# Two large gathers moved to the head of GpSimd's queue, and two more early groups with an announced jump

## The chip, the cores and the metric

One Trainium2 chip; the kernel runs on one of its cores. The metric is the device time of one execution in microseconds, the median of repeated runs. The engines are TensorE (PE, with PEld for its weight loads), VectorE (DVE), ScalarE (ACT), GpSimd (POOL) and SyncE (SP), which issues most of the DMAs.

## The reference, cut to what matters

Three stages follow one another. Attention (2 batches, 8 heads, 768 positions, 64 wide) gives 1536 tokens of 512 numbers. A mixture of experts works on these: a token with a positive skip score goes to the one expert of eight that its gate prefers, the others pass unchanged. A feed-forward block of 2048 hidden columns works on all tokens.

```python
do_compute = x @ w_skip > 0                  # tokens that go to an expert
e_idx = np.argmax(xc @ w_gate, axis=1)       # one of 8 experts each
h = np.maximum(xc[mask] @ w1[e], 0.0)        # 512 -> 1024
y[mask] = gate_w[mask, None] * (h @ w2[e])   # 1024 -> 512
out[do_compute] = xc + y
h = x @ w_in                                 # 512 -> 2048, all 1536 tokens
out = (h * np.cos(h)) @ w_out                # 2048 -> 512
```

## The kernel before

Attention writes its 1536 rows to a table `xb` in DRAM. The stage of the experts reads its rows from there and writes them back in place, and the feed-forward block reads the finished rows from there.

**Experts.** `CAP` is 32. The first 32 tokens of every expert are gathered as a small tile `xg` (`ex_gather`, 64 half rows). The next up to 64 are a tile `xo` (`ov_gather`, 64 rows), which is gathered for every expert whether it has them or not. An expert with more than 96 tokens has, instead, a tile `xm` of 128 rows (`many_gather`), which stands under a condition, since few experts are so large; one with more than 160 has both. All of these are indirect DMAs of GpSimd, which its queue issues in the order of the program. The weights (2 MB for each of an expert's two matrices, in four pieces) go through eight buffers; SyncE issues the pieces in order, each behind the landing of the third piece before it, and those ahead of the loop behind one gather each (`load_piece(ex_gather(...))`).

The loop over the experts is staggered: iteration `e` turns the hidden rows of expert `e` (`ex_t`), makes the first product of expert `e + 1` (`ex_w1`), turns the rows of expert `e + 2` (`ex_x`), then makes the second product of `e` (`ex_w2`), adds and scatters its rows (`ex_out`), and runs the larger tiles of `e` under their conditions (`overflow`, with `full_tile` for 128 rows and `part_tile` for 64). For every condition each engine reads the count into a register and branches.

**Work between the experts.** The table `WORK` puts steps of the next stage into the loop, under a letter for the place (`B` ahead of the second product, `J` behind the overflow, `A` behind that) and the number of the expert. Steps are named `c` (join the two halves of a weight chunk into float32, on ScalarE and VectorE), `sp` and `s` (split it into two parts for the product; the cast is on ScalarE, the subtraction on GpSimd for `sp` and on VectorE for `s`), `l` (load one), `yl` and `y` (gather 128 finished tokens and transpose them), and `f`, `b`, `d`: the three links of one early group of the feed-forward block. An early group is twelve products of 512 columns into one bank (`early_1`, then ScalarE and VectorE), a sine and a product (`early_2`), and a cast and a subtraction (`early_3`). `EARLY = 2` groups of the first four are in the loop.

**The jump.** Behind the loop stands `rest_all`, the code for tokens that fit in none of the tiles, with a second pass over the early groups (`again`). It is long, and with the given tokens every engine branches over it. Behind it the list `START` is run in order: the other two groups (`f_2 ... d_3`), the conversions `c_6`, `c_7`, `sp_6`, `s_7`, eight gathers of 128 finished tokens in final order (`yl_01234567`), four groups of the second product (`p_0` to `p_3`), and the transposes of the gathered tokens (`y_45`, `y_67`). The main loop follows, over four quarters of the hidden columns and three blocks of 512 tokens; its first step transposes token tile 8.

These lines set the order of the gathers ahead of the loop:

```python
for e in range(NE):
    if e + 2 < NE:
        load_piece(ex_gather(e + 2))
    load_piece(ov_gather(e))
    if e == 0:
        many_gather(0)
```

Of the kernel before, what the change touches and what calls it, by code (L numbers as in the profile page):

```python
# [41 lines left out]
MORE = {7: 1}  # L42
AHEAD = 3

START = "c_6 sp_6 yl_01234567 c_7 f_2 s_7 o p_0 b_2 f_3 d_2 p_1 b_3 d_3 y_45 p_2 y_67 v p_3"
EARLY = 2

WORK = {
    "S0": "order",
# [6 lines left out]
    "Z4": "l6",  # L56
    "J5": "y23 c4",
    "A5": "sp4 l7 c5",
    "B6": "f0 b0 f1",
    "A6": "d0 b1 sp5",  # L60
    "A7": "d1",
}
CV0 = 8
POOL_G = [(0, 1, 0), (0, 1, 1), (0, 1, 2), (0, 1, 3)]
# [51 lines left out]
def tile_kernel(ctx: ExitStack, tc: tile.TileContext, consts, qh, kh, vh, vw, w9, w1, w2, w_in, w_out, out):  # L116
# [62 lines left out]
    def load_piece(after=None, half=None):  # L179

        if not wq:
            return
        u, part = wq.pop(0) if half != 0 else wq[0]
        e, kind = divmod(u, 2)
        k, w = (4, w1) if kind == 0 else (8, w2)
        ks, fs = slice(part * k // 4, (part + 1) * k // 4), slice(None)
        if half is not None and kind == 0:
            fs = slice(512 * half, 512 * half + 512)
        elif half is not None:
            ks = slice(2 * part + half, 2 * part + half + 1)  # L190
        d = nc.sync.dma_start(out=wt[u].rearrange("p (k f) -> p k f", k=k)[:, ks, fs],
                              in_=w[e].rearrange("(k p) f -> p k f", p=P)[:, ks, fs])
        if after is None and len(pieces) >= AHEAD:
            after = pieces[-AHEAD]
        if after is not None:
            tc.add_manual_dep(d.ins, after.ins.name, SYNC, reason="pace")
        pieces.append(d)
# [692 lines left out]
    def cv_load(q, i, after=None):  # L890
        kind, j = divmod(i, 4)
        r = cvt.tile([P, 1024], I32, tag="raw", name="raw", bufs=3 if q == 0 else 2)
        if kind == 0:
            src = w_in[j * P:(j + 1) * P, q * 512:(q + 1) * 512].bitcast(I32)
        else:
            src = w_out[(4 * q + j) * P:(4 * q + j + 1) * P, :].bitcast(I32)
        d = nc.sync.dma_start(out=r, in_=src)
        if after is not None:
            tc.add_manual_dep(d.ins, after.ins.name, SYNC, reason="rows first")
        raws[q, i] = r  # L900
# [23 lines left out]
    def ex_gather(e):  # L924
        xg.append(m1.tile([QA, 256], F32, name=f"xg{e}"))
        return gather(xg[e], GIA[:, e:e + 1], xb2)
# [11 lines left out]
    def many_gather(e):  # L938
        cnts[e] = cnt(0, e, NTOK), nc.values_load(CNT[0:1, 2, e:e + 1], min_val=0, max_val=1, skip_runtime_bounds_check_because=why)
        xm[e] = m2.tile([P, DM], F32, tag="xm", name="xm")  # L940
        with tc.If(cnts[e][0] > CAP + YT):
            apart(gather(xm[e], GIB[:, e:e + 1], xb), None, ("m", e % 2))
# [210 lines left out]
    def rest_all():  # L1153

        w = [wpc.tile([P, 4096], F32, tag="w", name="wr") for _ in range(2)]
        x = m2.tile([P, DM], F32, tag="xm", name="xr")
        with tc.If(over(0)):  # L1157
            for e in range(NE):
                rest(e, w, x)
            again()  # L1160

    def over(e):
        return nc.values_load(FEW[0:1, e:e + 1], min_val=0, max_val=NLOOP + 1, skip_runtime_bounds_check_because=why) > 0
# [43 lines left out]
    early_f = {}  # L1207

    def early_1(i):
        p, u = early_f[i] = ((ps_h, ps_o)[i % 2].tile([P, 512], F32, tag="ho"[i % 2], name="pf"), xo[3 + 2 * i])  # L1210
        f1_mm((0, 0, i), p)
        f1_v(p, u, xo[4])

# [25 lines left out]
    def do(where, e):  # L1239
        for a in WORK.get(where + str(e), "").split():  # L1240
            kind = a.rstrip("0123456789")
            for i in a[len(kind):] or "0":
                acts[kind](int(i))
# [3 lines left out]
    load_w(7)  # L1247
    cv_load(0, 0, first_in)
    load_piece(first_in)
    for e in range(NE):  # L1250
        if e + 2 < NE:
            load_piece(ex_gather(e + 2))
        load_piece(ov_gather(e))
        if e == 0:
            many_gather(0)
        if e in (1, 3):
            cv_load(0, (e + 1) // 2)
    while wq:
        load_piece()
    do("S", 0)  # L1260
    for e in range(NE):
        ex_t(e)
        do("T", e)
        if e + 1 < NE:
            ex_w1(e + 1, ps_h.tile([P, 256], F32, tag="h", name="ph"), m2.tile([P, 256], F32, tag="h", name="h"))
        if e + 2 < NE:
            ex_x(e + 2)
        do("B", e)
        if e + 1 < NE:
            many_gather(e + 1)  # L1270
        po = ps_o.tile([P, 256], F32, tag="o", name="po")
        ex_w2(e, hs.pop(e), po)
        ex_out(e, po)
        overflow(e)
        do("J", e)
        if e == 4:
            cv_alloc(0, 0)
            t = wpa.tile([P, 2, 4, 512], F32R, tag="w", name="yb")
            Y[0] = (t[:, 0], t[:, 1])
        if e == 5:  # L1280
            gs.append(wpa.tile([P, 2, 4, 512], F32R, tag="w", name="g0"))
            cv_alloc(0, 1)
        do("A", e)
        for u in range(2 * e + NU, min(2 * e + 2 + NU, 2 * NE)):
            load_w(u)
        while wq:
            load_piece()
        do("Z", e)
# [176 lines left out]
```

## Time and profile before

| | |
|---|---|
| median of the runs | 494.01 us |
| lowest of the runs | 493.82 us |
| profiled execution, its own time | 495.81 us |
| its span, first to last instruction | 494.0 us |
| TensorE busy | 443.3 us (90%) |
| VectorE busy | 308.3 us (62%) |
| ScalarE busy | 213.7 us (43%) |
| GpSimd busy | 148.9 us (30%) |
| DMA read and written | 75.8 MB |

All times inside the program are counted from the span's first instruction. The busy shares are means over three stages that differ: attention to about 88 us, the experts to about 218 us, the feed-forward block to the end. A line number names a line of the kernel, often that of a helper.

### The profile page before, as it was taken

How to read it: one execution, taken by the hardware profiler on the slowest of the kernel's cores; microseconds unless marked ns; L12 is line 12 of the kernel's file. 1: busy time of each engine (PE TensorE's matmuls, PEld its weight loads, DVE VectorE, ACT ScalarE, POOL GpSimd, SP SyncE). 2: the span in 40 equal slices, each digit the busy share in tenths (PEclk: the TensorE clock that was granted, in tenths of full speed). 3: DMA queues.
4: the chain of work that ended last, by engine and by line, in shares of the span. 5: the costliest groups of instructions: out<-in, count | busy, mean ns of one | idle time of the engine just before them, and what ended most of it. 6: DMA issues, size and time to landing. Idle time of an engine off the chain costs nothing.

```text
span 494.0 us, 8759 instructions
## 1 busy us (share of the span) xinstructions
PE 443.3 (90%) x3037; PEld 331.9 (67%) x3037; DVE 308.3 (62%) x862; ACT 213.7 (43%) x518; POOL 148.9 (30%) x156
## 2 busy tenths in 40 slices
PE   6999998950999886948999999999999999999994
PEld 3878886520444342526888888888888888888883
DVE  4798998640051141465658797999889965563741
ACT  2988885100231130332646566644536433150600
POOL 3576652372120026125115232223123200003033
PEclk9999999985899998997999999999999999999997
DMA  9998986779979897103501322322132000002021
GB/s 238 300 306 294 341 300 235 230 248 304 350 255 317 308 325 278 57 12 100 181 23 47 124 85 86 126 86 88 55 116 85 1 1 0 1 0 75 12 104 67
DMA packets 36785, 76.09 MB, mean 154 GB/s; under 512 B 4249, under 2 KB 12955, under 8 KB 36724
## 3 DMA queue, kind: packets, MB, share of 16 engines
q1 hardware_dynamic: 33476, 66.07, 41.2%
q0 software_dynamic: 3248, 9.27, 5.6%
q8 instruction: 31, 0.51, 0.4%
q14 instruction: 30, 0.25, 0.2%
HBM read 68.15 MB, written 7.60 MB: 153 GB/s over the span
## 4 chain that ended last, share of the span: by engine, by line
PE 29%; issue 18%; DVE 3%; POOL 3%; POOLq 0%; ACT 0%; DVEq 0%; ACTq 0%
PE pf L1188 15%; PE py L1333 11%; POOL out L630 2%; PE py L1399 2%; DVE g L1204 1%; PE pt L1118 1%; DVE cvu L911 0%; DVE cvc L912 0%; DVE u L1194 0%; DVE c L1198 0%; POOL wx L920 0%; POOLq L1461 0%; DVE nn L1193 0%; DVE cvu L909 0%; ACT u L1192 0%
## 5 line engine op out<-in xcount | busy, mean ns | idle before, releaser
L1188 PE MATMUL pf<-yb,wx 128*128 128x512 f32 x576 | 136.3, 394 | 6.6 <-DVEq L1157 4.8
L1188 PEld LDWEIGHTS pf<-yb,wx 128*128 128x128 f32 x576 | 109.1, 190 | 30.4 <-issue 7.8
L1333 PE MATMUL py<-wx,g 128*128 128x512 f32 (+1 forms) x540 | 121.6, 384 | 0.0
L1333 PEld LDWEIGHTS py<-wx,g 128*128 128x128 f32 x540 | 99.9, 188 | 20.2
L1192 ACT ACTIVATE u<-pf,qbias 128x512 f32<-128x512 f32 x46 | 31.5, 684 | 86.7 <-PE pf L1188 82.7
L920 POOL TENSOR_TENSOR wx<-cvc,wx 128x512 fp32r<-128x512 f32 x24 | 34.7, 1445 | 94.7 <-ACT wx L919 91.5
L1204 DVE TENSOR_TENSOR g<-c,g 128x512 fp32r<-128x512 f32 x42 | 42.6, 1015 | 0.8 <-ACT g L1203 0.7
L1339 DVE TENSOR_TENSOR ya<-py,ya 128x512 f32<-128x512 f32 (+1 forms) x37 | 23.8, 671 | 28.2 <-PE py L1333 28.2
L340 ACT ACTIVATE sm<-sm,nm 128x128 f32<-128x128 f32 x96 | 37.5, 393 | 5.6 <-DVE nm L328 5.5
L1193 DVE TENSOR_SCALAR nn<-u 128x512 f32<-128x512 f32 x46 | 19.5, 424 | 30.6 <-ACT u L1192 30.6
L1197 ACT ACTIVATE c<-u 128x512 f32<-128x512 f32 x46 | 28.8, 627 | 17.5 <-DVE g L1204 16.1
L630 POOL DMA_INDIRECT out<-ya,PERM x11 | 10.9, 990 | 79.9 <-DVE ya L1339 79.3
L1194 DVE TENSOR_TENSOR u<-u,nn 128x512 f32<-128x512 f32 x46 | 31.9, 693 | 1.6
L1198 DVE TENSOR_TENSOR c<-pf,c 128x512 f32<-128x512 f32 x46 | 31.5, 684 | 0.9 <-ACT c L1197 0.7
L322 PE MATMUL ps<-kT,qbd 128*128 128x128 f32 x192 | 28.1, 296 | 3.3 <-DMA qbd<-qh 3.3
L350 POOL TENSOR_TENSOR sm<-sm,su 128x512 f32<-128x512 f32 x23 | 23.9, 1040 | 21.5 <-DVE su L349 10.8
L322 PEld LDWEIGHTS ps<-kT,qbd 128*128 128x128 f32 x192 | 26.1, 209 | 4.3 <-issue 4.1
L1203 ACT CAST g<-c 128x512 fp32r<-128x512 f32 x46 | 28.0, 608 | 1.0 <-DVE c L1198 1.0
L1059 DVE SCALAR_TENSOR_TENSOR xm<-pox,GTB,xm 128x512 f32<-128x512 f32 x2 | 1.5, 750 | 42.9 <-PE pox L1049 42.9
L328 DVE CUSTOM_DVE_ANT_0 sm<-ps,cst 128x128 f32<-128x128 f32 x96 | 23.7, 284 | 6.1 <-PE ps L322 6.1
L919 ACT CAST wx<-cvc 128x512 fp32r<-128x512 f32 x24 | 14.9, 622 | 16.4 <-DVE cvc L912 16.4
L979 PE MATMUL po<-w,hT 128*32 128x256 f32 x256 | 18.0, 429 | 3.5 <-ACTq L1169 1.9
(250 smaller groups left out, 631.5 us busy)
## 6 DMA issues: line engine op xcount, KB each, us to landing
w<-w SPq DMA_DIRECT2D x62, 512.0 KB, 5.9
raw<-w_in SPq DMA_DIRECT2D x16, 512.0 KB, 3.9
raw<-w_out SPq DMA_DIRECT2D x16, 512.0 KB, 3.3
kT<-kh SPq DMA_DIRECT2D x8, 384.0 KB, 6.5
vn<-vh SPq DMA_DIRECT2D x12, 256.0 KB, 5.2
xb<-xtok SPq DMA_DIRECT2D x12, 256.0 KB, 4.3
qd<-qh SPq DMA_DIRECT2D x4, 512.0 KB, 5.2
vt<-vw SPq DMA_DIRECT2D x12, 128.0 KB, 4.8
```

The costliest lines, as they stand in the source:

```text
L322: nc.tensor.matmul(ps[:, p, :], q[:, p, :, :].rearrange("p h (a t) -> p (h a) t", t=2)[:, :, t % 2], kT[b][:, p, k0:k0 + P], start=True, s ...
L340: nc.scalar.activation(out=sm[:, p, :], in_=sm[:, p, :], func=AF.Exp, scale=-1.0, bias=nm[:, p:p + 1], accum_out=su[:, p:p + 1])
L350: nc.gpsimd.tensor_tensor(out=sm, in0=sm, in1=su.unsqueeze(2).to_broadcast([P, NP, P]), op=ALU.mult)
L920: eng.tensor_tensor(out=lo, in0=c, in1=hi.bitcast(F32), op=ALU.subtract)
L1188: nc.tensor.matmul(p, w[:, k, fs], y[:, k, :], start=(n == 0), stop=(n == 11))
L1192: nc.scalar.activation(out=u, in_=p, func=AF.Identity, scale=1.0 / (2.0 * math.pi), bias=qbias)
L1194: nc.vector.tensor_tensor(out=u, in0=u, in1=nn, op=ALU.subtract)
L1197: nc.scalar.activation(out=c, in_=u, func=AF.Sin, scale=TWO_PI)
L1198: nc.vector.tensor_tensor(out=c, in0=p, in1=c, op=ALU.mult)
L1203: nc.scalar.copy(out=gh, in_=g)
L1204: (nc.gpsimd if i in POOL_G else nc.vector).tensor_tensor(out=gl, in0=g, in1=gh.bitcast(F32), op=ALU.subtract)
L1333: nc.tensor.matmul(p, a[:, ws], b[:, f, cs], start=(n == 0), stop=(n == 11))
```

## The change

Two edits. The gathers ahead of the loop get another order: the small tiles of experts 2, 3 and 4, then for experts 0 and 1 the conditional 128-row tile and behind it `xo`, then the others; `many_gather(1)` so moves out of iteration 0. And all four groups of the first early block, with the conversions of chunks 6 and 7 that stood with them, are placed in iterations 6 and 7 of the loop, ahead of the jump. The condition around `rest` gets a label, and ahead of the last `J` step every engine is given a hint that this branch will likely be taken. `f1` moves from iteration 6 to iteration 7. Groups 2 and 3 need a place for their results, `ysrc[0]` and `ysrc[1]`, whose tokens are transposed by then.

```diff
-START = "c_6 sp_6 yl_01234567 c_7 f_2 s_7 o p_0 b_2 f_3 d_2 p_1 b_3 d_3 y_45 p_2 y_67 v p_3"
-EARLY = 2
+START = "yl_01234567 o p_0 p_1 y_45 p_2 y_67 v p_3"
+EARLY = 4
...
-    "B6": "f0 b0 f1",
-    "A6": "d0 b1 sp5",
-    "A7": "d1",
+    "B6": "f0 b0",
+    "A6": "d0 sp5 c6",
+    "B7": "f1 b1",
+    "J7": "f2 d1 f3 sp6 b2 c7",
+    "A7": "d2 b3 s7 d3",
...
-        with tc.If(over(0)):
+        with tc.If(over(0), label="rest"):
...
-        p, u = early_f[i] = ((ps_h, ps_o)[i % 2].tile([P, 512], F32, tag="ho"[i % 2], name="pf"), xo[3 + 2 * i])
+        p, u = early_f[i] = ((ps_h, ps_o)[i % 2].tile([P, 512], F32, tag="ho"[i % 2], name="pf"), (xo[3], xo[5], *ysrc)[i])
...
-    for e in range(NE):
-        if e + 2 < NE:
-            load_piece(ex_gather(e + 2))
+    for e in range(2, 5):
+        load_piece(ex_gather(e))
+    for e in range(2):
+        many_gather(e)
         load_piece(ov_gather(e))
-        if e == 0:
-            many_gather(0)
-        if e in (1, 3):
-            cv_load(0, (e + 1) // 2)
+    for e in range(2, NE):
+        if e + 3 < NE:
+            load_piece(ex_gather(e + 3))
+        load_piece(ov_gather(e))
+        if e in (3, 5):
+            cv_load(0, (e - 1) // 2)
...
-        if e + 1 < NE:
+        if 0 < e < NE - 1:
             many_gather(e + 1)
...
         overflow(e)
+        if e == NE - 1:
+            tc.mark_branch_hint_location("rest", hint="LikelyTaken")
         do("J", e)
```

## Rows read from the trace of the kernel before

**Rows 1.** Stretches (us from start): length, busy time (instructions) by engine, clock, DMA share, GB/s
```profile
109.04:122.03 12.99, 0.00 (x1) 0.00 (x1) 0.85 (x2) 0.00 (x0) 4.22 (x5) 0.50 0.99 287
...
218.11:222.91 4.80, 0.01 (x2) 0.03 (x1) 1.65 (x3) 0.98 (x2) 1.96 (x2) 0.96 0.06 15
222.91:229.82 6.91, 5.07 (x13) 3.81 (x13) 4.24 (x6) 1.18 (x2) 3.50 (x3) 0.53 0.12 30
229.82:245.30 15.48, 15.48 (x78) 12.87 (x77) 9.09 (x15) 8.36 (x15) 5.70 (x6) 1.00 0.60 193
245.30:494.00 248.70, 241.57 (x1085) 200.39 (x1083) 180.75 (x284) 110.12 (x193) 53.10 (x41) 0.99 0.18 60
```

**Rows 2.** Timeline, 98 to 163 us: gathers and tiles of experts 1 and 2
```profile
98.95 0.90 POOL L626 DMA_INDIRECT xg<-xb,GIA  x1 [0.97 <-remote]
...
104.31 0.31 PE L604 MATMUL ptx<-ident,xg 64*128 64x64 f32 x2 [2.04 <-DMA xg<-xb,GIA]
...
113.52 0.97 POOL L626 DMA_INDIRECT xm<-xb,GIB  x1 [0.30 <-issue]
...
122.06 1.09 PE L995 MATMUL ptx<-ident,xm 128*128 128x128 f32 x4 [13.02 <-DMA xm<-xb,GIB]
122.79 0.95 POOL L630 DMA_INDIRECT xb<-xg,SIA  x1 [8.31 <-DMA xm<-xb,GIB]
...
124.93 0.97 POOL L626 DMA_INDIRECT xm<-xb,GIB  x1 [1.19 <-issue]
...
140.54 0.75 DVE L1059 SCALAR_TENSOR_TENSOR xm<-pox,GTB,xm 128x512 f32<-128x512 f32 x1 [30.62 <-PE pox L1049]
...
145.97 0.66 PE L995 MATMUL ptx<-ident,xm 128*128 128x128 f32 x4
...
162.49 0.75 DVE L1059 SCALAR_TENSOR_TENSOR xm<-pox,GTB,xm 128x512 f32<-128x512 f32 x1 [12.32 <-PE pox L1049]
```

**Rows 3.** Source line L626, 90 to 112 us: landing of the small gathers
```profile
DMA to landing us min/median/max: 3.3/5.8/8.7
```

**Rows 4.** Source line L191, 166 to 173.5 us: weight pieces, first and last issue, landing
```profile
L191 SPq DMA_DIRECT2D w<-w x6: 328/378/424, 166.1 to 172.9; - x6
...
DMA to landing us min/median/max: 3.2/4.2/5.9
```

**Rows 5.** Stretches again, for the DMA share and the clock
```profile
92.00:104.00 12.00, 9.70 (x162) 5.28 (x158) 7.72 (x44) 2.32 (x7) 4.73 (x6) 1.00 0.63 196
104.00:138.00 34.00, 18.95 (x77) 9.33 (x78) 1.39 (x3) 5.85 (x11) 10.90 (x12) 0.70 0.97 321
138.00:148.00 10.00, 8.85 (x96) 4.48 (x95) 6.58 (x16) 2.02 (x5) 3.70 (x5) 1.00 0.75 243
188.00:192.00 4.00, 3.61 (x33) 1.45 (x34) 0.00 (x0) 0.19 (x2) 1.46 (x3) 0.57 0.80 259
```

**Rows 6.** Timeline, 182 to 239 us: expert 6's product, early groups, the stretch behind the jump
```profile
182.32 1.91 PE L642 MATMUL ph<-w,xe 128*32 128x256 f32 x27
...
206.10 5.74 PE L1188 MATMUL pf<-yb,wx 128*128 128x512 f32 x24
...
225.65 1.28 POOL L920 TENSOR_TENSOR wx<-C,wx 128x512 fp32r<-128x512 f32 x1 [4.87 <-ACT wx L919]
227.08 1.26 POOL L626 DMA_INDIRECT ya<-xb,PERM  x1
...
235.50 0.69 ACT L1192 ACTIVATE u<-pf,qbias 128x512 f32<-128x512 f32 x1 [2.88 <-PE pf L1188]
...
238.03 1.04 PE L1118 MATMUL pt<-ident,ya 128*128 128x128 f32 x8
```

**Rows 7.** Tile `ya` on GpSimd, 227 to 231.5 us: landing of final rows
```profile
DMA to landing us min/median/max: 3.5/3.6/3.7
```

**Rows 8.** Source lines L1157 and L1169: TensorE's branches over `rest` and over an overflow (ns)
```profile
L1157 PEldq COMPARE_BRANCH  x1: 3700/3700/3700, 218.7 to 218.7; - x1
...
L1169 PEldq COMPARE_BRANCH  x2: 313/313/313, 212.2 to 216.6; - x2
```

## The prediction

> **What bounds the kernel now.** I read the stretches of the span first [rows 1], cut where the program passes from one step to the next. From 245.30 us on TensorE is busy 241.57 of 248.70 us: whatever makes the transposes of token tile 8 (the first thing after 245.30) start earlier, ends the program earlier by as much. So the question is what stands still ahead of them. Two holes show. From 109.04 to 122.03 TensorE does nothing, at a granted clock of 0.50. From 218.11 to 222.91, around the jump over `rest`, it does nothing again, and the stretch after it has 5.07 us of work in 6.91 at a clock of 0.53.
>
> The timeline names the first hole [rows 2]: expert 1's 128-row tile `xm` is what the transposes at 122.06 waited for, 13.02 us. Its gather was issued by GpSimd at 113.52, behind the small gathers of all eight experts, though nothing it needs came so late: the small gather that follows the first condition left at 98.95. Expert 3's rows, `xg`, also came late by 2.04 us, at 104.31.
>
> **Part one, the gathers.** In the new order GpSimd issues experts 2, 3 and 4's small gathers first, then `xm` of expert 0 (skipped), `xo` of 0, `xm` of 1, `xo` of 1, then the rest. `xo` of 0 keeps its place, since it waits for its list, so `xm` of 1 takes the slot of 98.95 [rows 2]. Gathers in this stretch land 3.3 to 8.7 us after issue, 5.8 in the middle [rows 3]: 102 to 107.7, taken 105. Expert 3's rows go out ahead of that, so the 2.04 us wait goes too, and TensorE stands ready for the tile at 109.04 - 2.04 = 107.0 instead of 122.06. That is 15.1 us. The tile itself, from its transposes to VectorE's last step, took 140.54 - 122.06 = 18.48 us after the hole and 162.49 - 145.97 = 16.52 us for expert 2, where the clock was full: another 2.0 us, which the hole's clock cost. Together 17.1, and 16.8 if the gather lands at the late end.
>
> What is late next? **Expert 2's tile** is gathered behind expert 0's scatter, and that scatter waits for every gather out of the same table to land: at 122.79 it follows the last one, and `xm` of 2 leaves 2.14 us later, at 124.93 [rows 2]. Twelve steps of the queue took 113.52 - 98.95 = 14.57 us, 1.21 each; with eleven gathers from 98.95 on, the last leaves at about 111.1, lands at 119.8 by the late end of [rows 3], the scatter goes at 120.7 and `xm` of 2 at 122.9; it lands between 128.7 and 131.6. TensorE wants it at 145.97 - 16.8 = 129.2. So the wait is 0 to 2.4 us; I take 0.8. **The expert weights** come next. The queue on SyncE issues them in order, each behind the landing of the third before it, and the first eleven behind a gather each; these gathers keep their rank within one place, so I cost that edit at nothing, up to 1 us. The four pieces of expert 6's first matrix were the first four of those issued from 166.1 us on, and pieces there landed within 5.9 us [rows 4], the fourth, issued near 169, by about 175; TensorE wanted them at 182.32 [rows 6]. That is 7 to 8 us of cover, less than 16. But the stream had holes of its own: idle DMA share of 0.37 in 92 to 104 (4.4 us), 0.03 in 104 to 138 (1.0 us), and 0.25 in 138 to 148 (2.5 us) [rows 5]; the last comes from buffers that the late tile held. Regained, 7.9 us, they make the cover 15 to 16. I take a wait of nothing here, bounds 0 to 8. Part one: **16 us**, between 8 and 17.1.
>
> **Part two, the early groups and the announcement.** All in the old frame, from the group that starts at 206.10; two groups took 5.74 us, one 2.87 [rows 6]. Group 0 ends at 208.97; expert 6's second product (1.9 us, the length of its first one [rows 6]) then no longer waits for group 1, and ends at about 211.3. Group 1 follows to about 214.7. Expert 7's second product needs its turned hidden rows copied by ScalarE, and in the new order that copy stands behind group 0's three passes and two steps of the conversions, each near 0.69 us [rows 6], with VectorE's links between them: about 215.9, so TensorE waits 1.2 us there. The product ends at 217.8, the skip over expert 7's overflow costs 0.31 [rows 8], and groups 2 and 3 end at 223.8, where the old program had not yet finished its first group behind the jump.
>
> What starts the rest is GpSimd. Its last conversion step, `sp6`, waits for a ScalarE cast which is queued behind group 3's pass: 223.8 + 0.69 + 0.69 + 1.28 = 226.5 [rows 6]. Then it jumps, and gathers tokens in the final order. The second gather goes some 1.6 us after the first (1.26 of issue and a pause of 0.30) and lands in 3.6 [rows 2, 6, 7]. If the announced jump costs no more than a short one, 0.3 to 0.7 us, the first gather leaves at 227.2 and two tiles are there at 232.4. TensorE meanwhile: jump, two `p` groups of 2.87 each, ready at 230 to 233. Then come the transposes (1.04 us each pair [rows 6]), `p_2`, transposes, `p_3`: 7.8 us, to 240.2, against 245.30. Gain 5.1 us. With TensorE as the only limit it would be 6.8; with GpSimd paying an unannounced fetch, 2.6 us more than that (the nearest row is TensorE's own, 3.70 us [rows 8]), about 2. A wait of 2 to 3 us in front of the transposes could lower the clock: after the hole before 188 us it stood at 0.57 for 4 us [rows 5], which costs at most 1.7. I take **5 us**, between 0 and 6.8. The conversions and scatters that move into the loop stand on VectorE and ScalarE beside TensorE's groups, and the sum above carries them through the copy and the cast that they delay; the announcement itself is one instruction on each engine and I cost it at nothing, up to the short branch's 0.31 us.
>
> The trace shows the jump's price on TensorE: 3.70 us for the branch over `rest`, 0.31 for the branches over an expert's overflow [rows 8]. The Trainium skill, page "Runtime: NRT & Kernel Launch", section "Instruction fetch mechanics", says that prefetch is purely sequential and that a taken branch to a target outside the current two-page window has to fetch the target first. The two prices agree with it; it speaks against the announcement, and it is the second rival.
>
> **The sum.** The profiled execution took 495.81 us with a span of 494.0; the median of the runs shown is 494.01, which is the span's size, so I subtract from 494.0. 494.0 - 16 - 5 = **473.0 us**.
>
> **Rivals.** First, *the weights take the place of the gather*: if the holes of the stream are not regained, the cover is 7 to 8 us and part one gives 8; with part two at 4 to 5, 481 to 482. For it: DMA at 0.97 from 104 to 138. Against: the holes were there because buffers were held. 0.15. Second, *the announcement does nothing*: every engine fetches the target at the jump as before, GpSimd's gathers leave at 230, part two gives 1 to 2, 476. By the page's rule this would be the outcome; the groups in front of the jump gain even so. 0.13. Third, *the change doesn't do what it says*: the gather ahead lands no sooner, because all gathers share one queue with the bytes of eleven others, and TensorE still waits to 118; part one gives 4 and part two 1 to 4, the time is 486 to 489. Against it are the landings of 3.3 to 8.7 us in issue order. 0.06. Fourth, *slower*: in place of one hole many short ones, in each of which the granted clock falls to 0.5, as it did in 109.04 to 122.03 and to 0.57 in 188 to 192. At half clock each us of product takes another us; TensorE has some 75 us of work between 122 and 218, and from 21 us of it at half clock on, the gain is gone. At 30 us the time is 503. Against: the stretches between the holes ran at full clock. 0.03.
>
> **How the numbers follow.** The forecast has 0.63. Its own range is 470 to 478: 494.0 less 17.1 and 6.8, and less 14 and 2. The stated range, 467 to 483, adds the first two rivals, and 3 us below for the hole ahead of 188 us, whose cause no row names and which may go. A difference of 2% (about what a measurement of this kernel can tell from no change) is 9.9 us, at 484.1: the forecast and the first two rivals lie below it, 0.91; the third lies mostly within 2%, 0.06; the fourth above, 0.03.
>
> **What would show it.** In the new profile: `xm` of expert 1 issued near 99 us and no wait for it over 1 us; a clock of 1.00 in the first tile and 16.5 us for it; expert 2's tile starting near 129; the stretch of the early groups with four `pf` groups ahead of the jump; TensorE's long branch down to some tenths of a us; the first gather of final rows near 211 (227 less 16); tile 8's transposes near 224. The prediction is wrong if weight pieces end waits of experts 3 to 7, if GpSimd's gathers after the jump leave later than the cast allows, or if the clock row falls between the experts.

## The result, and the profile after

The changed kernel takes **489.17 us** (median of 20 runs) beside 494.7 us of the kernel before (20 runs): ratio **0.9885**, 95% interval 0.9862 to 0.9907. 473.0 was forecast. Its profiled execution took 489.0 us with a span of 487.2, so it stands at the median, and against the span of before the gain is 6.8 us where 21 were forecast. In the changed kernel lines ahead of the loop stand two further down, lines of the last stage seven (L995 is L997, L1188 is L1190, L1157 is L1159, L1399 is L1406).

Stretches of the kernel after, cut at the same program points as [rows 1] (columns as there), answering to them and to [rows 5] for 104 to 138:

```profile
104.00:138.00 34.00, 30.33 (x176) 14.14 (x173) 10.34 (x26) 8.00 (x16) 11.98 (x15) 0.90 1.01 321
188.37:210.97 22.60, 18.15 (x150) 11.93 (x148) 16.69 (x26) 8.83 (x17) 5.27 (x5) 1.00 0.11 32
210.97:223.11 12.14, 0.00 (x1) 0.03 (x1) 6.38 (x10) 4.67 (x8) 1.73 (x1) 0.66 0.28 90
223.11:231.40 8.29, 8.29 (x26) 6.57 (x27) 0.00 (x0) 0.00 (x0) 5.73 (x7) 0.67 0.55 144
231.40:238.51 7.11, 7.11 (x41) 6.01 (x40) 3.57 (x6) 4.08 (x8) 1.87 (x2) 1.00 0.44 130
238.51:487.20 248.69, 241.58 (x1085) 200.44 (x1083) 180.67 (x284) 110.12 (x193) 53.02 (x41) 0.99 0.18 60
```

The main loop (the last row) is what it was, 248.69 us. From 104 to 138 TensorE is busy 30.33 us where it was busy 18.95. The hole at 109 is gone, and behind the early groups there is a new one: 12.14 us with one TensorE instruction in it, where the hole at the jump had 4.80, and the 24 products behind it take 8.29 us at a clock of 0.67.

Timeline of the kernel after, 98 to 134 us, which answers to [rows 2]:

```profile
98.58 0.96 POOL L628 DMA_INDIRECT xm<-xb,GIB  x1 [0.34 <-issue]
...
108.17 0.43 PE L997 MATMUL ptx<-ident,xo 64*128 64x64 f32 x4 [1.78 <-DMA xo<-xb,GIS]
...
108.53 0.66 PE L997 MATMUL ptx<-ident,xm 128*128 128x128 f32 x4
...
128.03 0.75 DVE L1061 SCALAR_TENSOR_TENSOR xm<-pox,GTB,xm 128x512 f32<-128x512 f32 x1 [18.97 <-PE pox L1051]
...
133.46 0.66 PE L997 MATMUL ptx<-ident,xm 128*128 128x128 f32 x4
```

Expert 1's tile was asked for at 98.58 and TensorE turns it at 108.53, with no wait for it and 1.78 us for `xo`. The tile ends with VectorE's step at 128.03. Expert 2's tile is turned at 133.46 and waited for nothing.

Timeline of the kernel after, 188 to 239 us, which answers to [rows 6]:

```profile
188.37 0.38 PE L969 MATMUL pth<-ident,h 128*128 128x128 f32 x2
...
190.55 3.01 PE L1190 MATMUL pf<-yb,wx 128*128 128x512 f32 x12
...
199.53 3.00 PE L1190 MATMUL pf<-yb,wx 128*128 128x512 f32 x12 [3.21 <-DVEq L1171]
...
205.22 5.75 PE L1190 MATMUL pf<-yb,wx 128*128 128x512 f32 x24 [0.83 <-ACTq L1171]
...
212.28 1.73 POOL L922 TENSOR_TENSOR wx<-C,wx 128x512 fp32r<-128x512 f32 x1 [4.35 <-ACT wx L921]
...
217.70 0.69 DVE L1206 TENSOR_TENSOR g<-xo,g 128x512 fp32r<-128x512 f32 x1
223.11 8.29 PE L1406 MATMUL py<-wx,g 128*128 128x512 f32 x24 [12.14 <-DVEq L1159]
223.84 0.98 POOL L628 DMA_INDIRECT ya<-xb,PERM  x1 [9.84 <-DMA raw<-w_in]
```

The row at 223.11 is the one to read: TensorE stood still for 12.14 us, and what ended that is VectorE at L1159, the condition around `rest`. GpSimd's last conversion was over at 214.01, its first gather of final rows left at 223.84.

Line L1159 of the kernel after, the branches over `rest` and the waits behind them (ns, first and last start), which answers to [rows 8]:

```profile
L1159 POOLq EVENT_SEMAPHORE  x5: 17/43/43, 215.5 to 215.9; - x5
...
L1159 ACTq EVENT_SEMAPHORE  x2: 17/17/17, 220.0 to 220.1; - x2
L1159 DVEq EVENT_SEMAPHORE  x2: 21/21/21, 222.9 to 223.1; - x2
...
L1159 PEldq COMPARE_BRANCH  x1: 3730/3730/3730, 207.4 to 207.4; - x1
L1159 POOLq COMPARE_BRANCH  x1: 45/45/45, 212.6 to 212.6; - x1
...
L1159 ACTq COMPARE_BRANCH  x1: 45/45/45, 217.4 to 217.4; - x1
L1159 DVEq COMPARE_BRANCH  x1: 56/56/56, 218.1 to 218.1; - x1
```

Each engine has its own jump. TensorE's takes 3.73 us as a branch and lies beside its own last products. On the others the branch is short and the time passes between it and the first wait behind it: GpSimd 212.6 to 215.5, ScalarE 217.4 to 220.0, VectorE 218.1 to 222.9. VectorE is the last to branch and the last to come out.

### The profile page after: what moved, and what is told of

The parts are those of the page before. It is cut to its first block, busy times and chain, and to the rows that moved or that the text cites. A ratio compares the mean times of both kernels' runs of the same rounds, so it can differ in the third digit from the quotient of the medians.

```text
span 487.2 us, 8759 instructions
## 1 busy us (share of the span) xinstructions
PE 444.2 (91%) x3035; PEld 331.3 (68%) x3037; DVE 308.5 (63%) x862; ACT 213.2 (44%) x518; POOL 148.2 (30%) x156
## 4 chain that ended last, share of the span: by engine, by line
PE 29%; issue 18%; DVE 3%; POOL 3%; POOLq 0%; ACT 0%; DVEq 0%; ACTq 0%
PE pf L1190 14%; PE py L1340 11%; PE py L1406 3%; POOL out L632 2%; DVE g L1206 1%; PE pt L1120 1%; DVE cvu L913 0%; DVE cvc L914 0%; DVE u L1196 0%; DVE c L1200 0%; POOL wx L922 0%; POOLq L1468 0%; DVE nn L1195 0%; DVE cvu L911 0%; ACT u L1194 0%
## 5 line engine op out<-in xcount | busy, mean ns | idle before, releaser
L1190 PE MATMUL pf<-yb,wx 128*128 128x512 f32 x576 | 134.2, 391 | 4.0 <-DVEq L1171 3.2
L1190 PEld LDWEIGHTS pf<-yb,wx 128*128 128x128 f32 x576 | 107.6, 188 | 27.3 <-issue 3.8
L1194 ACT ACTIVATE u<-pf,qbias 128x512 f32<-128x512 f32 x44 | 30.1, 684 | 80.3 <-PE pf L1190 80.2
L1206 DVE TENSOR_TENSOR g<-c,g 128x512 fp32r<-128x512 f32 x40 | 41.2, 1030 | 0.1
L1199 ACT ACTIVATE c<-u 128x512 f32<-128x512 f32 x44 | 27.6, 627 | 16.0 <-DVE g L1206 16.0
L1196 DVE TENSOR_TENSOR u<-u,nn 128x512 f32<-128x512 f32 x44 | 30.5, 692 | 1.5
L1200 DVE TENSOR_TENSOR c<-pf,c 128x512 f32<-128x512 f32 x44 | 30.0, 683 | 0.7 <-ACT c L1199 0.7
L1205 ACT CAST g<-c 128x512 fp32r<-128x512 f32 x44 | 26.7, 608 | 0.2 <-DVE c L1200 0.2
L1406 PE MATMUL py<-wx,g 128*128 128x512 f32 x48 | 14.3, 460 | 12.1 <-DVEq L1159 12.1
```

What stands on the lines that cost most here:

```text
L1190: nc.tensor.matmul(p, w[:, k, fs], y[:, k, :], start=(n == 0), stop=(n == 11))
L1194: nc.scalar.activation(out=u, in_=p, func=AF.Identity, scale=1.0 / (2.0 * math.pi), bias=qbias)
L1196: nc.vector.tensor_tensor(out=u, in0=u, in1=nn, op=ALU.subtract)
L1199: nc.scalar.activation(out=c, in_=u, func=AF.Sin, scale=TWO_PI)
L1200: nc.vector.tensor_tensor(out=c, in0=p, in1=c, op=ALU.mult)
L1205: nc.scalar.copy(out=gh, in_=g)
```

## The experiments

Two numbers are read from each trace: when expert 6 begins (its transposes), which shows part one, and the **stretch** from there to tile 8's transposes, which shows part two whatever the start did. Ratios are against runs of the kernel before on the same chip in the same set of runs. Sets 1 and 3 ran on the same chip, the other sets on three others. Each start and stretch is from one trace.

| set, kernel | groups ahead of the jump | expert 6 begins | tile 8 | stretch | median, ratio [95%] |
|---|---|---|---|---|---|
| before | 2 | 203.92 | 245.30 | 41.38 | 494.7 |
| after | 4 + conversions | 188.37 | 238.51 | 50.14 | 489.17, 0.9885 |
| 1 gathers alone | 2 | 187.08 | 229.70 | 42.62 | 480.55, 0.9677 [0.9626, 0.9728] |
| 1 early groups alone | 4 + conversions | 201.74 | 252.33 | 50.59 | 504.75, 1.0192 [1.0135, 1.0250] |
| 1 register hint | 4 + conversions | 187.68 | 239.22 | 51.54 | 489.65, 0.9868 [0.9833, 0.9903] |
| 1 no `rest` | 4 + conversions | 189.54 | 233.94 | 44.40 | 485.35, 0.9796 [0.9754, 0.9838] |
| 2 conversions behind | 4 | 203.39 | 250.89 | 47.50 | 501.93, 1.0121 [1.0056, 1.0187] |
| 2 three early | 3 | 206.75 | 250.44 | 43.69 | 499.92, 1.0099 [1.0063, 1.0135] |
| 2 gathers, no `rest` | 2 | 203.47 | 239.70 | 36.23 | 490.68, 0.9898 [0.9827, 0.9969] |
| 2 block hint | 4 + conversions | 205.33 | 255.83 | 50.50 | 506.39, one run |
| 3 gathers again | 2 | 205.58 | 248.34 | 42.76 | 498.56, 1.0059 [1.0020, 1.0098] |
| 3 change again | 4 + conversions | 206.65 | 258.52 | 51.87 | 505.98, 1.0175 [1.0113, 1.0238] |
| 3 three again | 3 | 207.15 | 252.86 | 45.71 | 500.49, 1.0083 [1.0047, 1.0118] |
| 3 before | 2 | 202.39 | 243.43 | 41.04 | 493.94, one run |
| 4 gathers, control | 2 | 185.82 | 229.86 | 44.04 | 480.59, 0.9731 [0.9688, 0.9774] |
| 4 one piece | 2 | 197.34 | 240.00 | 42.66 | 494.50, 0.9997 [0.9958, 1.0036] |
| 4 gathers later | 2 | 197.97 | 240.40 | 42.43 | 489.56, 0.9881 [0.9850, 0.9911] |
| 4 shifted code | 2 | 193.13 | 234.52 | 41.39 | 484.82, 0.9773 [0.9723, 0.9824] |
| 5 vector load | 4 + conversions | 185.52 | 236.86 | 51.34 | 492.10, 0.9944 [0.9906, 0.9982] |
| 5 three, control | 3 | 187.57 | 231.01 | 43.44 | 481.75, 0.9753 [0.9694, 0.9811] |

**The two parts apart.** The gathers alone is the kernel before with the gathers' loop and the condition on `many_gather` of the change; the early groups alone is the changed kernel with the old gathers' order.

> Only the new order of the gathers; the early groups and the jump as in the kernel before. Theory A (the gathers gain their 15.5 us, seen in the changed kernel as 203.92 to 188.37 at expert 6, and the second part gives 9 us of it back): 494 - 15.5 = 478 to 479 us, faster than both kernels. Rival B (the gathers' gain is mostly eaten further on whatever stands behind the loop, and the second part is neutral): 488 to 490 us, like the changed kernel.

> Only the second part: four early groups in the loop and the announcement as it stands in the change; gathers in the old order. Theory A: 494 + 9 = 502 to 504 us, slower than the kernel before. Rival B: 493 to 495 us.

480.55 and 504.75: the gathers alone beat both kernels, the early groups alone lose to the kernel before. Part two is a loss with either order of the gathers: in the stretch 8.0 us within set 1 (42.62 to 50.59), in the time 8.8 us beside the kernel before of that set (495.98).

**The announcement.** The instruction listing of the changed kernel has no added instruction on any engine in front of the branch: the announcement, written with a label and no engines, made none, and its trace holds none. Two kernels carry a real one, the first with a register's value for its hint, the second (its edit follows) with a fixed hint in a block of its own.

```diff
-            tc.mark_branch_hint_location("rest", hint="LikelyTaken")
+            with tc.block():
+                tc.mark_branch_hint_location("rest", hint="LikelyTaken", engines=list(mybir.ALL_ENGINES))
```

> The changed kernel, with the announcement given a register (the same count that the branch tests), which puts a hint instruction on every engine's stream at that place; in the change as it stands no engine's stream holds one for this branch. Theory A (the announcement was not there, and a real one shortens each engine's jump from 2.6 to 4.8 us to under 1 us): VectorE passes the join some 4 us sooner, 484 to 486 us. Rival C (a hint cannot help, the target has to be fetched at the jump all the same): 489 us, branch on TensorE still 3.7 us.

> The changed kernel with the announcement put into a block of its own and given to all engines, so that an instruction of it stands in every engine's stream ahead of the third early group. Theory A: a jump's price isn't changed by this announcement: TensorE's branch over the rest stays at 3.7 us and GpSimd's at 2.6 or more, the time is 489 to 492 (the block adds a join). Rival B: the announcement with a fixed target works where the one with a register did not: branches under 1 us on every engine, the second product starts 3 to 4 us sooner, 484 to 486.

Line L1159 of the second, block hint:

```profile
L1159 ACTq EVENT_SEMAPHORE  x2: 17/17/17, 236.4 to 236.5; - x2
L1159 DVEq EVENT_SEMAPHORE  x2: 21/21/21, 241.5 to 241.6; - x2
...
L1159 PEldq COMPARE_BRANCH  x1: 3729/3729/3729, 225.9 to 225.9; - x1
...
L1159 ACTq COMPARE_BRANCH  x1: 68/68/68, 236.0 to 236.0; - x1
L1159 DVEq COMPARE_BRANCH  x1: 74/74/74, 236.7 to 236.7; - x1
```

ScalarE's jump fell from 2.6 us to 0.4 (with the register hint too), TensorE's stayed at 3.73 and VectorE's at 4.8. Since VectorE comes out last, nothing is gained: 489.65 for the register hint, and a stretch of 50.5 for the block. With the register hint the announcement ran 2.3 us ahead of the branch on TensorE, 10.8 on VectorE and 11.9 on ScalarE; why it shortened ScalarE's jump alone isn't shown.

**The jump taken out.** The code for tokens that fit in no tile is left out, first of the change (no announcement either), then of the gathers alone.

```diff
-    rest_all()
```

> The changed kernel without the code for tokens that fit in no tile (nothing of it runs with these tokens), so that no condition and no join stand between the loop and what follows; the announcement goes with it. Theory A (what is behind the join waits until VectorE has run all its early work and jumped, TensorE idle 12.1 us): TensorE's second products start right behind group 3, the first final gather leaves at 214 to 218.5 instead of 223.8, 477 to 483 us. Rival D (ScalarE's and VectorE's chain of the four groups is itself too long, the join only shows it): 487 to 489 us.

> The new order of the gathers with two early groups, without the code for tokens that fit in no tile (left out, so that no jump and no join stand there). With four early groups ahead of the jump, leaving that code out was worth some 4 us. Theory A: with two groups ahead and two behind it the hole at the jump (4.8 us, and 1.8 us more in the stretch behind it) goes for the most part: 480.6 less 5 to 8, 473 to 476. Rival B: TensorE waits there for banks and tiles that the next stage uses again, jump or not: 478 to 481. If A holds, this is what the announcement could have brought at the most.

With four early groups the stretch falls by 5.7 us, with two by 6.4. The time of the first, 485.35, lies between its two theories; the second's, 490.68, is far over the 473 to 476 of theory A, because its expert 6 began at 203.47, while its stretch fell by what that theory says. Timeline rows of the change without `rest`, behind the early groups:

```profile
219.44 7.24 PE L1403 MATMUL py<-wx,g 128*128 128x512 f32 x24 [6.11 <-DVE xo L1200]
...
221.54 0.98 POOL L628 DMA_INDIRECT ya<-xb,PERM  x1 [5.17 <-DVE g L1206]
```

Without a jump TensorE still waits 6.11 us, now for VectorE's last reading of the fourth group's bank (`xo`, L1200), which the next stage uses again. VectorE's jump in the changed kernel took 4.8. So of the 12.14 us about half is VectorE's chain behind the last group and half its jump.

**How many groups.** Three early groups (on the gathers alone) put the third behind expert 7's overflow and leave the fourth and the conversions behind the jump; the other kernel keeps four and moves the conversions behind.

```diff
-START = "c_6 sp_6 yl_01234567 c_7 f_2 s_7 o p_0 b_2 f_3 d_2 p_1 b_3 d_3 y_45 p_2 y_67 v p_3"
-EARLY = 2
+START = "c_6 sp_6 yl_01234567 c_7 f_3 s_7 o p_0 b_3 d_3 p_1 y_45 p_2 y_67 v p_3"
+EARLY = 3
...
-    "A7": "d1",
+    "J7": "f2 d1",
+    "A7": "b2 d2",
```

```diff
-START = "yl_01234567 o p_0 p_1 y_45 p_2 y_67 v p_3"
+START = "yl_01234567 c_6 s_6 c_7 s_7 o p_0 p_1 y_45 p_2 y_67 v p_3"
...
-    "A6": "d0 sp5 c6",
+    "A6": "d0 sp5",
...
-    "J7": "f2 d1 f3 sp6 b2 c7",
-    "A7": "d2 b3 s7 d3",
+    "J7": "f2 d1 f3 b2",
+    "A7": "d2 b3 d3",
```

(The second edit also moves the subtraction of chunk 6 from GpSimd, `sp6`, to VectorE, `s_6`.)

> The changed kernel without the announcement, and with the conversions of chunks 6 and 7 (two ScalarE casts, one GpSimd and one VectorE subtraction, two joins of halves) put back behind the jump, all four early groups still ahead of it. Theory A: the join behind the jump waits for the slowest engine's early work, VectorE's last step at 217.70 and its jump of 4.8 us, so taking away what VectorE does there (two joins of halves of 1.81 us and a subtraction of 0.69, together 4.3 us) lets the first group of the second product start some 4 us sooner than 223.1: about 219, and the time is near 485. Rival B: the jump is what costs, and the early work's order on VectorE doesn't matter: the time stays near 489. Rival C: the conversions that stand behind the jump again become what the second product waits for, up to 5 us: 490 to 494.

> The new order of the gathers with three early groups in the loop (the third behind the overflow of expert 7), the fourth and the conversions behind the jump as before. Two groups gave 480.6, four with the conversions gave 489.2. Theory A: each group put ahead of the jump brings its ScalarE and VectorE links ahead of the join, so that what TensorE gains ahead of the jump (2.87 us a group) it waits behind it: 480 to 483. Rival B: a group that is moved forward saves its own 2.9 us, and only the fourth group or the conversions lose: 476 to 478.

> Three early groups in the loop, the fourth and the conversions behind the jump. In its first trace the stretch from expert 6 to token tile 8 took 40.5 us, 2.1 less than with two groups. Theory A: the third group forward is a gain of its own, and the loss of the change comes from the fourth group and the conversions in front of the jump: about 2 us shorter than the gathers alone on the same chip. Rival B: no difference, the 2 us are within what one profile differs from another.

> Three early groups in the loop with the fourth and the conversions behind the jump, once more. Theory A: the stretch from expert 6 to token tile 8 is again near 40.5 to 41 us (the gathers alone: 42.6 to 42.8), so that where TensorE's slow stretch at 107 us is absent the time is 478 to 480, just below the gathers alone (480.6), and 499 to 500 where it is there. Rival B: the 2 us were chance: 481 to 483.

The 40.5 in two of these texts is a misreading: the transposes at 247.22 are tile 7's, tile 8's follow at 250.44, so three groups have 43.7, 45.7 and 43.4. In the stretch: two groups 42.6 to 44.0 (three traces of the gathers alone), three 43.4 to 45.7, four with the conversions behind 47.5, four with all 50.1 to 51.9. The third group moved forward saves nothing; the fourth and the conversions cost, by one trace with the conversions behind. In set 5 three groups took 481.75, beside 480.55 and 480.59 of the gathers alone in others. The conversions' own 2.6 us are under the 4 that were expected, because VectorE finished no sooner: its last early step ended 30.1 us behind the start of expert 6, in the changed kernel 30.0. Timeline rows of the kernel with the conversions behind:

```profile
221.80 5.73 PE L1190 MATMUL pf<-yb,wx 128*128 128x512 f32 x24 [0.81 <-ACTq L1171]
...
232.83 0.69 DVE L1206 TENSOR_TENSOR g<-xo,g 128x512 fp32r<-128x512 f32 x1 [0.68 <-ACT g L1205]
...
236.33 7.04 PE L1404 MATMUL py<-wx,g 128*128 128x512 f32 x24 [8.79 <-DVEq L1159]
```

VectorE's links of the last group end 6.0 us behind TensorE's (233.52 against 227.53): a chain of ScalarE and VectorE steps of 0.4 to 0.7 us that no product covers any more. Then comes its jump, 2.9 us here (233.2 to 236.2) in place of 4.8. That is 1.9 of what the conversions' move saved; the 24 products behind the wait took 7.04 us in place of 8.29.

**VectorE made later.** Six idle steps of 0.69 us on VectorE alone, behind its last early step and ahead of the jump.

```diff
+    for _ in range(6):
+        nc.vector.tensor_tensor(out=xo[4], in0=xo[4], in1=xo[4], op=ALU.subtract)
     rest_all()
```

> The changed kernel with six idle VectorE steps of 0.69 us each (4.1 us, on a tile that nobody reads any more) behind its last early step, ahead of the jump. Theory A: behind the jump TensorE's first product waits for VectorE, for its last early step and its own branch, so it starts some 4 us later, the stretch from expert 6 to token tile 8 grows from 50.1 to about 54 us, and the time by 4 us (493 where the changed kernel has 489). Rival B: it waits for GpSimd's conversion, ScalarE or TensorE's own branch, and VectorE has slack: the stretch stays within 1 us of 50.

Timeline of it, then its line L1159:

```profile
215.46 4.32 DVE L1297 TENSOR_TENSOR xo<-xo 128x512 f32<-128x512 f32 x6
222.49 7.27 PE L1408 MATMUL py<-wx,g 128*128 128x512 f32 x24 [14.38 <-DVEq L1159]
```

```profile
L1159 DVEq EVENT_SEMAPHORE  x2: 21/21/21, 222.3 to 222.4; - x2
...
L1159 DVEq COMPARE_BRANCH  x1: 56/56/56, 219.5 to 219.5; - x1
```

TensorE's wait grew from 12.14 to 14.38 us, by 2.2, and it still ends 0.2 us behind VectorE's coming out. In the five traces with four groups, the conversions and no idle steps the wait was 12.10 to 12.16, so the growth is no scatter. The added 4.3 us came through by half, because VectorE's jump shrank from 4.8 to 2.8 us. The stretch is 51.34, 1.2 more than after and inside the 50.1 to 51.9 of such kernels; the ratio rose from 0.9885 (and 0.9868 with the register hint) to 0.9944. So VectorE ends the wait, and the size of its jump isn't constant; the stretch met neither theory A's 54 nor rival B's 50 within 1. What sets the size of VectorE's jump isn't shown.

**The start in other sets.** All four kernels of set 2 began expert 6 at 203 to 207 us, as late as the kernel before.

> The new order of the gathers alone, the same kernel that gave 480.6 (0.968). Four later kernels with this order had, all of them, a stretch from about 107 to 119 us in which TensorE did the second product of expert 0 one instruction every 0.7 us, and their expert 6 began at 203 to 207 us in place of 187 to 190. Theory A: that comes from where and when the kernels run, not from what is in them, so the gathers' gain is there in one place and lost in another: either 478 to 482 as at first with expert 6 at 187, or 492 to 496 with the same slow stretch at 107. Rival B: the slow stretch comes from what these four kernels changed behind it, and this one is again near 480 wherever the four are slow.

> The changed kernel itself beside the gathers alone on the same chip. From the start of expert 6 to token tile 8 it took 50.1 us, the gathers alone 42.6. Theory A: it is 7 to 9 us longer than the gathers alone in the same set of runs, whatever the start does: about 489 beside 480, or 503 beside 495. Rival B: the two differ by less than 3 us once they run side by side.

> The kernel before, for a trace on the same chip. Theory A: if the new order's kernels show the slow stretch at 107 to 119 us here, this one doesn't show it or hides it under its own wait for the 128-row tile, 13 us from 109, and its expert 6 begins near 204 us as in its first trace. Rival B: it is slower by the same 12 us, near 506, and the new order keeps its gain beside it.

The same file that took 480.55 us took 498.56 on the same chip, more than the 492 to 496 that theory A gave for a slow place. Part two's loss stayed beside it (505.98). TensorE's rows in expert 0's second product, gathers again in set 3, then that stretch as a window:

```profile
106.61 1.48 PE L979 MATMUL po<-w,hT 128*32 128x256 f32 x19
...
111.52 0.38 PE L979 MATMUL po<-w,hT 128*32 128x256 f32 x1 [0.87 <-issue]
112.91 0.57 PE L979 MATMUL po<-w,hT 128*32 128x256 f32 x1 [1.01 <-issue]
114.34 0.58 PE L979 MATMUL po<-w,hT 128*32 128x256 f32 x1 [0.86 <-issue]
```

```profile
108.10:121.10 13.00, 5.37 (x13) 1.11 (x13) 0.01 (x1) 0.54 (x2) 7.08 (x8) 0.69 0.96 275
```

Products that follow one another at once start 1.4 us apart, each with a weight load between, 0.7 us an instruction, and what they wait for is "issue": nothing that the trace shows. In set 1 the same instructions of the same file ran at 101.03, 2.54 us for all of them and no gap, at a DMA share of 1.01 (101 to 103.6 us); from 106 to 109.4 us it did expert 1's second product, with one gap of 0.65 us at a share of 0.97. The kernel before, in set 3:

```profile
111.64 0.58 PE L979 MATMUL po<-w,hT 128*32 128x256 f32 x1 [0.83 <-issue]
...
117.22 3.90 PE L979 MATMUL po<-w,hT 128*32 128x256 f32 x26 [1.50 <-issue]
...
122.92 0.64 PE L995 MATMUL ptx<-ident,xm 128*128 128x128 f32 x4 [1.19 <-DMA xm<-xb,GIB]
```

It has the slow stretch at the same time, but in expert 1's second product, and loses nothing by it: the tile came only at 122.9, and its wait of 13.02 us [rows 2] shrank to 1.19. Set 4 was to find the cause: with less traffic of weights, with fewer gathers, and with the code moved by 48 tiny products at the start, all on the gathers alone.

```diff
+    def one_piece(d):
+        load_piece(pieces[-1])       # each piece behind the one before it
...
-            load_piece(ex_gather(e + 3))
-        load_piece(ov_gather(e))
+            one_piece(ex_gather(e + 3))
+        one_piece(ov_gather(e))
```

```diff
-        load_piece(ov_gather(e))
+        if e < 3:
+            load_piece(ov_gather(e))
...
         if 0 < e < NE - 1:
             many_gather(e + 1)
+            if e > 1:
+                apart(ov_gather(e + 1), None, ("o", e + 1))
```

```diff
-    warm(ps_s, "s", 18)
+    warm(ps_s, "s", 18, 48)          # 18 products of 512 columns, then 48 of 8
```

> The gathers alone once more, as the kernel beside which the three others of this set are read: 480 if the slow stretch on TensorE near 107 to 119 us is absent, 498 if it is there.

> The gathers alone, with one weight piece at a time from the ninth gather on up to the loop, in place of three (each piece waits for the one before it): the DMA traffic between 104 and 122 us falls, and the weights of later experts come later. Theory A: TensorE's slow stretch (one instruction each 0.7 us) comes from the DMA traffic there: it shrinks from 12 us to under 4, expert 0's second product ends near 110; later waits for weights of 3 to 12 us take some of it back. Rival B: it doesn't come from the traffic: the stretch stays 12 us long and the later waits are added, over 500.

> The gathers alone, with the 64-row gathers of experts 3 to 7 moved into the loop, an iteration ahead of their expert: five indirect gathers fewer between 104 and 116 us, the weights' traffic as before. Theory A: the indirect gathers are what slows TensorE there: the slow stretch goes, 484 to 488 where the control has 498, or 480 where the control has 480. Rival B: the weights' traffic or something else does it: the slow stretch stays, within 3 us of the control.

> The gathers alone with 48 more tiny products in the warm-up at the very start, where TensorE waits for its first data: every later TensorE instruction stands 96 instructions further on in the program. Theory A: the slow stretch belongs to a place in TensorE's instruction stream (its instructions come one by one behind a boundary): it moves to other instructions, 96 earlier in the stream, or goes. Rival B: it belongs to the time from 107 us on, or to the work of other engines: it stays in expert 0's second product, within 3 us of the control.

The control was at 480.59 and no kernel of set 4 had the slow stretch, so its cause is not told apart. What the three showed is something else. With one weight piece at a time the second product of expert 2 started at 139.14, after 11.71 us of waiting for ScalarE. ScalarE itself had stood still ahead of this step of the next stage's conversions, whose load is in the same queue behind the pieces:

```profile
138.16 0.67 ACT L907 ACTIVATE C<-raw 128x512 f32<-128x512 f32 x1 [7.99 <-DMA raw<-w_in]
```

With the small gathers in the loop, that of expert 5's `xo` left at 178.01 and TensorE waited 9.50 us for it. The kernel shifted by 96 instructions, with the same work behind them, took 4.2 us more by the median (484.82 beside 480.59), but the intervals of the two ratios overlap, so the times alone don't show a cost. Waits of TensorE in one trace each, from 155 us to the end of the loop, first of the control and then of the shifted kernel (us in total, times, longest):

```profile
PE ph L642 <- issue: 1.0, 1, 1.0
...
PE pt L1118 <- PEq L1169: 0.4, 1, 0.4
```

```profile
PE pt L1119 <- PEq L1170: 3.6, 1, 3.6
PE ph L643 <- issue: 1.7, 1, 1.7
```

The gap moved from expert 6's first product to expert 5's, and the wait behind the branch over expert 4's overflow grew from 0.4 to 3.6 us. That fits a wait set by the place in TensorE's program; two traces don't prove it.

## Why the prediction was right and wrong

**Part one was right in its size**, 15.55 us (expert 6 at 188.37 in place of 203.92) where 16 were taken, but in part by luck: two of its terms were off and cancel. The gather left at 98.58 and the tile was turned at 108.53, 1.5 us later than the 107.0 forecast, because `xo` of expert 1 was waited for. The clock's 2.0 us weren't regained: the clock was at 0.67 in 112 to 118 us, while expert 1's tile ran, and the tile took 19.50 us (108.53 to 128.03) where 16.52 were forecast and 18.48 had been needed before. Expert 2's tile was turned at 133.46, with no wait, where 130.0 was the sum. That is 12.51 us in place of 16. (In the sum, a landing at the late end, 107.7, leaves 16.4 of the 17.1 and not 16.8.) The other 3.04 came from the hole ahead of 188 us, for which the range had an allowance: in expert 6's first product the gap fell from 2.68 to 1.29 us, and the product behind it ran at full clock, 1.93 us in place of 3.61:

```profile
173.06 0.63 PE L644 MATMUL ph<-w,xe 128*32 128x256 f32 x6 [1.29 <-issue]
...
174.53 1.93 PE L981 MATMUL po<-w,hT 128*32 128x256 f32 x32 [0.57 <-ACT xe L607]
```

No weight piece ended a wait, so the rival of the weights didn't come. But all this holds for the runs of the result and for sets 1, 4 and 5. In sets 2 and 3 expert 6 began 16 to 20 us later, and the gathers alone gave 1.006. Some 12 of these us lie in the slow stretch. Others lie ahead of it: ScalarE's copy for expert 0's first product (`cst<-ptx`) ran at 94.5 to 98.6 us in the seven traces of the new order there, at 91.4 to 94.3 in all other traces; what it waited for isn't known. No rival had that in it.

**Part two was wrong**, 8.8 us lost (stretch 41.38 to 50.14) where 5 were to be gained, and this is nearly the whole miss: 13.8 of the 14.2 us between 473.0 and the span of 487.2. The step that failed is "What starts the rest is GpSimd ... TensorE meanwhile: jump, two `p` groups of 2.87 each, ready at 230 to 233". In the prediction's frame (later by 15.55) the products started at 238.7 and were ready at 247. What starts the rest is VectorE: in 17 of the 18 traces that have the jump, the profile puts the end of TensorE's wait down to VectorE, and the first product starts 0.2 us or less behind VectorE's coming out. (In the shifted kernel, where the two came out together, it is put down to TensorE's own branch.) The row was there to be read; this one of the kernel before was passed over:

```profile
222.91 1.19 PE L1188 MATMUL pf<-yb,wx 128*128 128x512 f32 x2 [4.79 <-DVEq L1157]
```

The prediction read TensorE's branch, 3.70 us [rows 8], as the price. With two groups ahead of the jump the two can hardly be told apart, as the waits behind the same condition show in the kernel before:

```profile
L1157 POOLq EVENT_SEMAPHORE  x5: 17/42/43, 223.4 to 223.7; - x5
...
L1157 PEldq EVENT_SEMAPHORE  x2: 51/51/51, 222.5 to 222.6; - x2
L1157 DVEq EVENT_SEMAPHORE  x2: 21/21/21, 222.7 to 222.9; - x2
```

TensorE was out of the jump at 222.6, VectorE at 222.9. GpSimd, which the sum waited for, came out at 223.4, behind TensorE's first product at 222.91, and in none of the eight traces with the jump and two groups ahead of it did it come out before that product. So TensorE doesn't wait for all engines here; that it waits for VectorE because VectorE reads the banks that the next products write fits the run without `rest`, and is argued.

Term by term. (a) VectorE's last step and its jump were not in the sum at all, that is, put at nothing without a reason: four groups ahead of the jump make its chain the last thing, 7.4 us behind TensorE's last product (218.39 against 210.97), and its jump to 222.9 follows; with two groups behind the jump that chain lies under their products. (b) "The conversions and scatters that move into the loop stand on VectorE and ScalarE beside TensorE's groups": they do, and they are queued ahead of VectorE's passing of expert 6's overflow, so that group 1 started 3.21 us late and groups 2 and 3 ended at 226.5 in the old frame, 223.8 forecast. (c) The lowered clock behind the wait was priced at 1.7 at most; the 24 products took 8.29 us in place of 5.74. (d) "If the announced jump costs no more than a short one": no announcement was in the program, and a real one shortened ScalarE's jump alone. In the changed kernel the jump took each engine 2.6 to 4.8 us, and in all 18 traces a 16 KB packet of the DMA queue q8, one of two that carry instructions, started 1.0 to 1.6 us into TensorE's branch. The page "Runtime: NRT & Kernel Launch" of the Trainium skill, section "Instruction fetch mechanics", says that a taken branch out of the current window stalls for its target; the trace agrees. The second rival was right that the announcement does nothing, but gave 476, because it too let TensorE wait for GpSimd's gathers alone.

**What stays open** is the slow stretch of sets 2 and 3. It is not a fixed place in the program (expert 0's product in one kernel, expert 1's in the other, both from about 107 to 120 us), not the DMA share by itself (0.96 with it, 0.97 without), and not the order of the gathers, as before has it too. Nor is it the chip, since sets 1 and 3 had the same. That instructions reach TensorE late fits the even 0.7 us and the waits of the shifted kernel, and is argued, not shown. One record speaks against its simplest form: in gathers again (set 3) q8, which moves one packet for some 240 of TensorE's instructions in the main loop and is taken for its queue by that, started packets at 100.5 and 124.8 us and none between. TensorE took its instructions without gaps again ahead of the second, a product of 32 steps in 2.60 us from 121.80. As far as this record goes, the stretch was no wait for a packet on its way. The best kernel is the gathers alone, 0.968 and 0.973 in two sets; in the third it is no faster than before.

## What to carry to other kernels

Behind a condition the first instruction of an engine can wait for another engine to come out: here TensorE's waited for VectorE, and not for GpSimd, which came out later still. So cost a jump by when each engine whose work that instruction needs reaches it, with that engine's own jump added. Read which one it is from the wait of the first instruction behind the jump, not from the branch of the engine that you care about. Work moved ahead of a jump must leave something with products behind it that covers the last group's chain on the other engines; moving the last group forward uncovers it. A gain that removes a wait is safe only if the wait hid nothing else in that stretch: trace the kernel before in more than one set of runs.

## What the runs showed of the hardware

- A jump over a long body cost each engine its own time: TensorE 3.3 to 4.0 us, GpSimd 2.5 to 3.0, ScalarE 2.4 to 3.1, VectorE 2.8 to 3.7, and 4.8 in all five kernels with the conversions in front of it; six more VectorE instructions brought it back to 2.8. An instruction that announces the branch took ScalarE's to 0.4 and left the others. In all 18 traces a 16 KB packet of an instruction queue (q8) started 1.0 to 1.6 us into TensorE's branch.
- The same kernel can have a stretch in which TensorE takes an instruction every 0.7 us for some 12 us, in whole sets of runs and not in others, with 18 us on the median (480.55 and 498.56).
- With 96 more tiny instructions at the program's start, TensorE's waits some 160 us later stood at other places and were 3.9 us longer in sum (1.4 and 5.3, one trace each); the medians differ by 4.2 us, with intervals that overlap.
